# The load of x issued ahead of the opening barrier in a decode block

## Chip, cores, metric

The kernel runs on 1 core of one Trainium2 chip. The metric is the device time of one execution in microseconds (us). Runs within 1.5% of the fastest of their kernel count as fast runs.

## The reference

One decode step of a transformer block for two sequences, cut to what matters: attention with a cache of 8192 positions and 32 heads of 128, then a gated feed-forward layer.

```python
x = A_x                                                   # 2 x 1 x 512, bfloat16
h = x + attention(layernorm(x), k_cache, v_cache, wq, wo) # each cache 2 x 32 x 8192 x 128
return h + ffn(layernorm(h), W_gate, W_up, W_down)
```

The two caches are 268 of the 281 MB that the kernel reads. x is 2 KB, wq is 4 MB, and q = layernorm(x) @ wq is needed before any score can be computed.

## The kernel before

SyncE issues all big loads, in one queue, one after the other: wq, a piece of wo, K(0), V(0), K(1), V(1) and so on, 8 MB each, and at the end the feed-forward weights. The load of wq already stands ahead of the opening barrier, at which the five engines (SyncE, ScalarE, VectorE, TensorE and GpSimd) wait for one another after GpSimd has filled some constants. Each engine reports there with an instruction called a drain (in the trace of this kernel the last one, SyncE's, ends at 0.57 us, and the engines go on at 0.72 to 0.73); a small helper moves the instruction there in the built program. The load of x is issued by ScalarE behind the barrier.

```python
def ahead_of_barrier(emit, engine):
    block = nc.cur_bb.bb.instructions
    n = len(block)
    emit()
    new = block[n:]
    del block[n:]
    at = next(i for i, x in enumerate(block)
              if isinstance(x, mybir.InstDrain) and x.engine == engine)
    block[at:at] = new

ahead_of_barrier(lambda: nc.sync.dma_start(
    V[:, SLOT:], A_wq.rearrange("(p c) n -> p (c n)", c=DC)).then_inc(sem_wq, 16), nc.sync.engine)
nc.scalar.dma_start(x_row, A_x[:, 0]).then_inc(sem_x, 16)
nc.sync.dma_start(
    wo_rows, A_wo[128 * DR:].rearrange("(p r) n -> p (r n)", r=4)).then_inc(sem_wl, 16)
load(K, A_k_cache, 0, k_sem[0])
# ... GpSimd fills constants, among them:
pool.run(nc.gpsimd.memset(place, 0.0))                 # 128 x 2048
# ... VectorE, the layer norm of x:
dve.wait((sem_x, 16))
dve.run(nc.vector.bn_stats(out=bst[:], in_=x_row))
# ...
t_ln = dve.run(nc.vector.tensor_scalar(                # 2 x 512, the normalised x
    out=lnx_row, in0=x_row, scalar1=mv[:, 0:1], scalar2=sd[:, 0:1],
    op0=ALU.subtract, op1=ALU.mult))
# ... TensorE transposes x, VectorE copies it out (t_xlT), then q = layernorm(x) @ wq:
pe.wait((sem_wq, 16), t_xlT, t_zero)
# ... after the q matmuls (t_q), V(0) may overwrite wq:
sp.wait(t_q)
load(V, A_v_cache, 0, v_sem)
```

The softmax here doesn't subtract the row's maximum and nothing guards it: scores larger than these inputs give would overflow.

Of the kernel before, what the change touches and what calls it, by code (L numbers as in the profile page):

```python
# [39 lines left out]
def bass_sequential_preLN__gqa_block_cached__glu_gated_reglu__decode_kernel(  # L40
# [39 lines left out]
    with ExitStack() as es:  # L80
        def S(name):
            return es.enter_context(nc.semaphore(name))
# [17 lines left out]
        sem_x, sem_wq, sem_wl, sem_out = S("x"), S("wq"), S("wl"), S("out")  # L100
# [26 lines left out]
        x_row = kT[0][0:B, 0:D]  # L127
# [49 lines left out]
        if True:  # L177

            def program():
# [5 lines left out]
# [9 lines that stand above are left out]

                ahead_of_barrier(lambda: nc.sync.dma_start(
                    V[:, SLOT:], A_wq.rearrange("(p c) n -> p (c n)", c=DC)).then_inc(sem_wq, 16), nc.sync.engine)
                nc.scalar.dma_start(x_row, A_x[:, 0]).then_inc(sem_x, 16)
                nc.sync.dma_start(
                    wo_rows, A_wo[128 * DR:].rearrange("(p r) n -> p (r n)", r=4)).then_inc(sem_wl, 16)
                load(K, A_k_cache, 0, k_sem[0])  # L200
# [642 lines left out]
                nc.sync.wait_ge(sem_out, 16 * B)  # L843

            program()

    return nc
# [28 lines left out]
```

## Time and profile before

| | before |
|---|---|
| median of 6 runs beside the changed kernel | 656.74 us (656.60 to 657.23) |
| span of the profiled run | 655.6 us |
| bytes read from HBM, and their rate over the span | 281.05 MB, 429 GB/s |
| x landed, as VectorE saw it | 7.0 us |
| wq landed | 12.2 us |
| K(0) landed | 34.4 us |

The span is counted from the first instruction of the program; the time of an execution is about 1.2 us longer. x, wq and K(0) land in this order. The lines that carry this are in the prediction below. In them SPq and ACTq are loads being issued by SyncE and ScalarE; PE is TensorE (PEld its loads of weights), DVE VectorE, ACT ScalarE and POOL GpSimd; a bracket gives how long the engine was idle just before, and what ended that. Three dots mark rows left out. Two rows of the timeline that it doesn't show matter later (start, length, engine, line, operation): before the change, VectorE's TENSOR_SCALAR, the last step of the layer norm, ran beside GpSimd's copies, after GpSimd's memset (a fill with zeros) of 128x2048 had ended.

```profile
6.11 1.80 POOL L234 MEMSET prod<- 128x2048 bf16 x1
...
8.53 0.63 DVE L252 TENSOR_SCALAR kT<-kT,mv,sd 2x512 bf16<-2x512 bf16 x1
```

### The profile page before, as it was taken

How to read it: one execution, taken by the hardware profiler on the slowest of the kernel's cores; microseconds unless marked ns; L12 is line 12 of the kernel's file. 1: busy time of each engine (PE TensorE's matmuls, PEld its weight loads, DVE VectorE, ACT ScalarE, POOL GpSimd, SP SyncE). 2: the span in 40 equal slices, each digit the busy share in tenths (PEclk: the TensorE clock that was granted, in tenths of full speed). 3: DMA queues.
4: the chain of work that ended last, by engine and by line, in shares of the span. 5: the costliest groups of instructions: out<-in, count | busy, mean ns of one | idle time of the engine just before them, and what ended most of it. 6: DMA issues, size and time to landing. Idle time of an engine off the chain costs nothing.

```text
span 655.6 us, 8544 instructions
## 1 busy us (share of the span) xinstructions
PE 373.4 (57%) x3481; PEld 238.7 (36%) x3481; DVE 432.9 (66%) x275; ACT 304.7 (46%) x719; POOL 88.9 (14%) x96
## 2 busy tenths in 40 slices
PE   2374573747457374645638555474745637574677
PEld 0151441515234161523416143351614325151445
DVE  2187593947849395783939669393975939488771
ACT  1364362725536173453717445371653627254460
POOL 4000020030302103030120303003030300303000
PEclk9866557565665656566565656656565565657566
DMA  9999999999999999999999999999999999999997
GB/s 416 445 444 393 444 444 440 400 444 444 448 400 440 444 444 436 404 444 444 444 408 436 444 444 432 408 444 444 444 396 444 444 444 436 408 444 422 432 414 310
DMA packets 6324, 281.16 MB, mean 429 GB/s; under 512 B 710, under 2 KB 812, under 8 KB 1324
## 3 DMA queue, kind: packets, MB, share of 16 engines
q1 hardware_dynamic: 6308, 281.05, 99.4%
q8 instruction: 5, 0.08, 0.1%
q14 instruction: 3, 0.02, 0.0%
q10 hardware_dynamic: 8, 0.00, 0.0%
HBM read 281.05 MB, written 0.00 MB: 429 GB/s over the span
## 4 chain that ended last, share of the span: by engine, by line
DMA 64%; PE 24%; ACT 7%; DVE 4%; issue 1%; SPq 0%; DVEq 0%; ACTq 0%
DMA K<-in_A_k_cache_dram 59%; PE T L406 17%; ACT kT L589 7%; DMA V<-in_A_v_cache_dram 5%; PE S L389 5%; DVE prod L572 1%; DVE X L572 1%; PE O L429 1%; DVE X L563 1%; DVE prod L563 1%; DVE scores L577 0%; PE S L775 0%; PE O L775 0%; PE O L827 0%; ACT e L517 0%
## 5 line engine op out<-in xcount | busy, mean ns | idle before, releaser
L589 ACT ACTIVATE kT<-T 128x1024 bf16<-128x1024 bf16 x160 | 160.2, 1023 | 199.0 <-PE T L406 195.1
L406 PE MATMUL T<-ident_f,K 128*128 128x128 f32 x640 | 165.8, 424 | 100.4 <-DVEq L609 95.0
L563 DVE TENSOR_TENSOR X<-K,q_c 128x11264 bf16<-128x11264 bf16 x15 | 90.4, 6026 | 173.1 <-DMA K<-in_A_k_cache_dram 173.1
L429 PE MATMUL O<-V,e 128*16 128x512 bf16 x1024 | 116.0, 590 | 112.4 <-ACT e L517 79.6
L406 PEld LDWEIGHTS T<-ident_f,K 128*128 128x128 f32 x640 | 117.9, 217 | 102.6 <-DVEq L609 97.1
L572 DVE TENSOR_TENSOR prod<-prod 128x5632 bf16<-128x5632 bf16 (+1 forms) x68 | 104.3, 1533 | 4.0
L563 DVE TENSOR_TENSOR prod<-K,q_c 128x11264 bf16<-128x11264 bf16 x17 | 102.3, 6019 | 6.2 <-DMA K<-in_A_k_cache_dram 4.5
L517 ACT ACTIVATE e<-scores 32x88 bf16<-32x88 f32 x128 | 51.0, 399 | 103.2 <-DVEq L620 101.5
L429 PEld LDWEIGHTS O<-V,e 128*16 128x16 bf16 x1024 | 30.0, 115 | 184.5 <-ACT e L517 103.1
L572 DVE TENSOR_TENSOR X<-X 128x5632 bf16<-128x5632 bf16 (+3 forms) x60 | 92.0, 1533 | 3.7
L389 PE MATMUL S<-q_c,kT 128*128 128x8 bf16 x1280 | 60.9, 171 | 38.5 <-ACT kT L589 38.5
L389 PEld LDWEIGHTS S<-q_c,kT 128*128 128x128 bf16 x1280 | 52.0, 107 | 74.3 <-ACT kT L589 72.4
L544 POOL MEMSET O_l<- 128x32 bf16 x13 | 1.7, 131 | 427.7 <-DVEq L626 427.7
L549 POOL COPY rsel<-rows 128x112 bf16<-128x112 bf16 x14 | 40.4, 2885 | 39.6 <-DVEq L626 38.7
L442 PE MATMUL Ob<-sel,os_sb 128*128 128x4 f32 x136 | 27.7, 327 | 11.0 <-ACT os_sb L592 11.0
L517 ACT ACTIVATE e<-S 32x40 bf16<-32x40 f32 x128 | 31.9, 249 | 2.4 <-PE S L389 0.9
L442 PEld LDWEIGHTS Ob<-sel,os_sb 128*128 128x128 f32 x136 | 26.2, 287 | 13.3 <-ACT os_sb L592 13.2
L517 ACT ACTIVATION_READ_ACCUMULATOR e<-scores 32x1 f32 x128 | 28.0, 218 | 0.0
L517 ACT ACTIVATION_READ_ACCUMULATOR e<-S 32x1 f32 x128 | 25.6, 200 | 1.5
L551 POOL TENSOR_TENSOR O_l<-O_cur,mask 128x32 bf16<-128x32 bf16 x14 | 23.1, 1652 | 0.0
L560 POOL COPY q_c<-q_all 128x144 bf16<-128x144 bf16 x16 | 15.2, 951 | 44.6 <-PE O L429 33.6
L589 ACT ACT_TABLE_LOAD x15 | 19.2, 1283 | 0.3
(106 smaller groups left out, 137.8 us busy)
## 6 DMA issues: line engine op xcount, KB each, us to landing
K<-in_A_k_cache_dram SPq DMA_DIRECT2D x2, 4096.0 KB, 21.4
V<-in_A_wq_dram SPq DMA_DIRECT2D x1, 4096.0 KB, 12.2
V<-in_A_v_cache_dram SPq DMA_DIRECT2D x1, 4096.0 KB, 24.9
X<-in_A_wo_dram SPq DMA_DIRECT2D x1, 3584.0 KB, 18.0
V<-in_A_v_cache_dram SPq DMA_DIRECT2D x1, 3072.0 KB, 31.9
K<-in_B_W_up_dram SPq DMA_DIRECT2D x1, 1376.0 KB, 29.6
K<-in_B_W_gate_dram SPq DMA_DIRECT2D x1, 1376.0 KB, 32.5
V<-in_A_v_cache_dram SPq DMA_DIRECT2D x1, 1024.0 KB, 33.9
```

What stands on the lines that cost most here:

```text
L389: i = nc.tensor.matmul(Sp[p % 2][:, A * jj:A * jj + 2 * A], lhsT=kv_[:, k, r, :], rhs=q_c[:, 2 * A * r:2 * A * r + 2 * A], start=(r == 0), ...
L406: i = nc.tensor.transpose(Tp[g % 2][:, k * 128:(k + 1) * 128], k_t[:, j:j + 2, :].rearrange("p j d -> p (j d)").bitcast(F32), ident_f[:])
L429: i = nc.tensor.matmul(Op[0][c:c + 16, :], lhsT=e_t[q][:, j // VJ, :], rhs=v_t[:, j:j + VJ, :].rearrange("p j d -> p (j d)"), start=(q == ...
L442: i = nc.tensor.matmul(Ob[:, 0:A], lhsT=os_sb[:, jj * Dh:(jj + 1) * Dh], rhs=sel[:, A * jj:A * jj + A], start=(jj == 0), stop=(jj == VJ - 1))
L517: i = nc.scalar.activation(out=e_t[q][h, j0 // VJ:j1 // VJ, :].rearrange("p g (j a) -> p g j a", a=A)[:, :, :, a], in_=src(h, a), func=ACT ...
L544: pool.run(e.memset(o_window(o - 1)[0], 0.0))
L549: e.tensor_copy(out=rsel[:, :, o % B, :], in_=bass.AP(x.tensor, x.offset, [list(x.ap[0]), [DR - OS, A], [1, DR]]))
L551: e.tensor_tensor(out=w, in0=O_cur[:].unsqueeze(2).broadcast_to([128, A, NM]), in1=mask[:, off // 4:off // 4 + OS // 4 * (A - 1) + 1:OS // ...
L560: nc.gpsimd.tensor_copy(out=q_c[:], in_=q_all[:, o]).then_inc(g2d, 1)
L563: return nc.vector.tensor_tensor(out=pr[:, 0:JC, :], in0=tile(K, p)[:, 0:JC, :], in1=q_c[:, Q2:QW].unsqueeze(1).broadcast_to([128, JC, Dh] ...
L572: run(nc.vector.tensor_tensor(out=pr[:, 0:JC, 0:w], in0=pr[:, 0:JC, 0:w], in1=pr[:, 0:JC, w:2 * w], op=ALU.add))
L589: to_pe(nc.scalar.activation(out=kT[gg % 2][:], in_=Tp[gg % 2][:].bitcast(BF16), func=ACT.Copy))
```

## The change

The intent: x should go out at the same time as wq, not 0.8 us later, so that the layer norm is done earlier. The whole diff:

```diff
-                nc.scalar.dma_start(x_row, A_x[:, 0]).then_inc(sem_x, 16)
+                ahead_of_barrier(
+                    lambda: nc.scalar.dma_start(x_row, A_x[:, 0]).then_inc(sem_x, 16), nc.scalar.engine)
```

## The prediction

The forecast's sum is 656.6 us: the 656.61 us of the kernel before, with 0 from x, 0 from the barrier and at most 0 to 0.1 us for a later first packet of wq. A rival by which the issue of x delays that of wq, for an end at 656.8 to 657.0 us, is the +0.4 in the range. Of the sum, 0 to 0.1 us is the author's estimate, with no measurement behind it. The packet records are of the kernel before.

> **What bounds the kernel now.** I read the page's slices first, then the chain that ended last at its two ends, then the opening in order of time, and last the waits of the first 35 us. The page of the kernel before:
>
> ```profile
> span 655.6 us, 8544 instructions
> ...
> DMA  9999999999999999999999999999999999999997
> ...
> DMA 64%; PE 24%; ACT 7%; DVE 4%; issue 1%; SPq 0%; DVEq 0%; ACTq 0%
> ```
>
> The DMA row is 9 in 39 of 40 slices, the first included: one stream of loads runs from the start to almost the end, and the chain that ended last is DMA for 64%. Most of its other links only decide when the next load is issued. The chain at both ends of the loop:
>
> ```profile
> 1.19 33.17 DMA K<-in_A_k_cache_dram
> ...
> 47.34 25.73 DMA K<-in_A_k_cache_dram
> ```
>
> ```profile
> 551.14 25.16 DMA K<-in_A_k_cache_dram
> ...
> 608.73 31.88 DMA V<-in_A_v_cache_dram
> ```
>
> The columns are start, length, what. The first block of K lands at 1.19+33.17 = 34.36 us, the fifteenth at 551.14+25.16 = 576.30, so one of the 14 rounds between them takes 541.94/14 = 38.71 us. A round loads 8 MB of K and 8 MB of V, 16,777,216 bytes, which makes 433.4 GB/s. The loads keep ahead: V(0) is issued at 15.9, K(0) lands at 34.36, and 8 MB at that rate take 19.4 us, so V(0) lands near 53.7, while K(1) is already issued at 47.34. Each next load stands in the queue some 6 us before the one ahead of it is done. So the end is: the start of the stream, plus its bytes at 433 GB/s, plus the tail of TensorE and VectorE work after the last V has landed at 608.73+31.88 = 640.6, which is 15.0 us. The change can move the end through the start of the stream, through a break in it, or through the tail.
>
> The opening in order of time (start, length, engine, line, operation):
>
> ```profile
> 0.00 0.40 SPq L195 DMA_DIRECT2D V<-in_A_wq_dram  x1
> ...
> 0.80 0.34 SPq L198 DMA_DIRECT2D prod<-in_A_wo_dram  x1
> 0.80 0.55 ACTq L197 DMA_DIRECT2D kT<-in_A_x_dram  x1
> 1.19 0.46 SPq L182 DMA_DIRECT2D K<-in_A_k_cache_dram  x1
> ...
> 2.00 1.03 DVE L229 MEMSET O<- 128x512 f32 x2
> ...
> 7.01 0.68 DVE L242 BATCH_NORM_STATS2 bst<-kT 2x6 f32<-2x512 bf16 x1 [3.98 <-DMA kT<-in_A_x_dram]
> ...
> 9.74 0.17 DVE L265 COPY xlT<-T 128x16 bf16<-128x16 bf16 x1 [0.58 <-PE T L261]
> ...
> 12.26 3.58 PE L276 MATMUL O<-V,xlT 128*2 128x512 bf16 x32 [2.56 <-DMA V<-in_A_wq_dram]
> ...
> 24.20 0.10 PEld L362 LDWEIGHTS Ob<-ident,onesn 128*128 128x128 bf16 x1
> ```
>
> The load of wq goes out at 0.00, before the barrier; the load of x after it, at 0.80. VectorE waits 3.98 us for x. The normalised, transposed x is ready at 9.74+0.17 = 9.91, but TensorE starts the q matmuls only at 12.26, when wq has landed. And the last piece of the opening, at about 24.4, waits in turn for K. The waits of the first 35 us say the same:
>
> ```profile
> DVE X L563 <- DMA K<-in_A_k_cache_dram: 14.7, 1, 14.7
> ...
> DVE bst L242 <- DMA kT<-in_A_x_dram: 4.0, 1, 4.0
> ...
> PE O L276 <- DMA V<-in_A_wq_dram: 2.6, 1, 2.6
> ```
>
> The wait for x (4.0 us) lies inside the wait for wq, which ends later by 2.4 us, and that lies inside the wait for K, which ends later by 10 us.
>
> [...] its packet records show the two 1 KB packets of x at 5.27 and 5.37 us, 46 ns each, between 32 KB packets of wq of 1,213 ns, and the two 4-byte semaphore writes at 6.52 and 6.62, one more wq packet later. [...] both issues of 0.80 start together, the one on SyncE takes 0.34, that of the tiny x 0.55.
>
> **The change, part by part.** Nothing is added or removed. On ScalarE the x issue moves from behind the wait on the barrier to the place ahead of its drain; the other four engines keep their order, which the built order of both programs confirms.
> (1) ScalarE reaches its drain at 0.13 us in the trace, so x is issued at about 0.13 instead of 0.80, 0.67 us earlier. [...] I take the whole issue as the 0.55 us of today: done at about 0.68. [...]
> (2) The barrier. Today SyncE's drain is the last to end, at 0.57, and the engines leave at 0.72 to 0.73. ScalarE's drain now ends at 0.68 plus up to the 0.12 that SyncE's drain takes: 0.7 to 0.8. The engines should leave 0.1 to 0.25 us later, near 0.9, and the loads of wo and K with the first GpSimd memset come later by as much. The stream doesn't see it: wq's 4 MB keep the DMA engines busy to about 12.3, and the K issue at 1.19 has some 11 us of room. The GpSimd constants end at 9.5 and their last use begins at 19.8.
> (3) x's packets. wq's first packets start at 1.02 us, 1.0 us after their issue began. [...] with none to two wq packets ahead of them instead of three, and perhaps one before the semaphore write. At 1.2 us a packet x lands at 2 to 5 us, middle 3.5, against 7.01. VectorE is free at 3.03, so BATCH_NORM_STATS2 starts at about 3.5 and xlT is ready at 3.5+2.9 = 6.4, 3.5 us earlier.
> (4) What follows: the q matmuls still start at 12.26, since they need all of wq. The 3.5 us won become 3.5 us more of TensorE waiting. V(0) is issued at 15.9, K lands at 34.4: unmoved.
> (5) x's 2 KB at 433 GB/s are 5 ns, before and after.
> Sum on the path that sets the end: 0 from x, 0 from the barrier, and at most the delay of wq's first packet, which I put at 0 to 0.1 us. Predicted: 656.6 us.
>
> **The rivals.** [...] *The chain from x matters after all*: if the opening set the end, 3.5 us would be won, 653.1 us. Against it are two waits that end later, with 2.4 and 10 us of slack. *The barrier costs*: if a stage after it were tight, 0.1 to 0.25 us would be added, 656.8. Against it: nothing after the barrier is used within 10 us of being tight to the stream, save the x chain itself. *The time outside the span*: 656.61 is timed and 655.6 is the span; an earlier ScalarE instruction could shift what is counted by 0.1 us either way.
>
> **Range and chances.** The three runs before lie within 0.11 us, the profiled one read 656.9. The modelled effects are 0 to +0.4, and I allow 0.5 us for another chip: 656.1 to 657.1. A gain or loss of 2% is 13 us, which no part of the opening could give or take without breaking the stream. Faster 0.005, within 2% 0.985, slower 0.01.
>
> **What would show it right or wrong.** Right: the x issue starts near 0.1 us; the wait of BATCH_NORM_STATS2 shrinks from 3.98 us to under 2; the wait of the q matmuls for wq grows from 2.6 to about 6; they still start at 12.2 to 12.4; K(0) lands at 34.3 to 34.5 and the rounds keep 38.71 us. Wrong on a size: x lands as late as before, so its place among the packets isn't set by its issue time. Wrong as a whole: wq's landing moves by over 0.3 us, or the end moves without it.

## The result, and the profile after

The changed kernel took 656.73 us (median of 6 runs, 656.47 to 657.03), the kernel before 656.74 us in the same rounds. The ratio is 0.9999, with a 95% interval of 0.9986 to 1.0012. All ratios here are the mean time of one kernel's fast runs over that of the other's of the same rounds, so not quite the ratio of the medians quoted. The time is the same; the program, read from its page, is as full of loads as it was:

```profile
span 655.3 us, 8543 instructions
...
DMA  9999999999999999999999999999999999999997
```

The span is 0.3 us shorter here, but the spans of the six runs lie between 655.2 and 655.7, so this is scatter. What moved is in the opening. The timeline of the changed kernel:

```profile
0.00 0.40 SPq L195 DMA_DIRECT2D V<-in_A_wq_dram  x1
0.12 0.55 ACTq L198 DMA_DIRECT2D kT<-in_A_x_dram  x1
...
1.10 0.34 SPq L199 DMA_DIRECT2D prod<-in_A_wo_dram  x1
...
4.74 0.68 DVE L243 BATCH_NORM_STATS2 bst<-kT 2x6 f32<-2x512 bf16 x1 [1.42 <-DMA kT<-in_A_x_dram]
...
6.26 2.07 DVE L253 TENSOR_SCALAR kT<-kT,mv,sd 2x512 bf16<-2x512 bf16 x1
6.39 1.80 POOL L235 MEMSET prod<- 128x2048 bf16 x1
...
8.91 0.17 DVE L266 COPY xlT<-T 128x16 bf16<-128x16 bf16 x1 [0.58 <-PE T L262]
...
12.16 3.21 PE L277 MATMUL O<-V,xlT 128*2 128x512 bf16 x32 [3.29 <-DMA V<-in_A_wq_dram]
```

x is issued at 0.12 instead of 0.80 and seen at 4.74 instead of 7.01, so the early issue bought 2.27 us of arrival for 0.68 us of issue. The barrier opens 0.3 us later: the load of wo is issued at 1.10 instead of 0.80, because ScalarE comes to the barrier later (its drain starts at 0.72 instead of 0.13). Of the 2.27 us only 0.83 are left when the transposed x is ready (9.08 instead of 9.91), because one TENSOR_SCALAR now takes 2.07 us instead of 0.63. And none is left at the q matmuls: they start when wq has landed, at 12.16 against 12.26. The gain has turned into waiting, as TensorE's wait for wq says: 3.29 us in the last row against 2.56 before. The load of K(0), on the chain that ended last, is issued 0.3 us later and lands no later:

```profile
1.49 32.69 DMA K<-in_A_k_cache_dram
```

K(0) landed at 34.17 after and 34.37 before the change, K(1) at 72.89 and 73.07.

### The profile page after: what moved, and what is told of

It is laid out like the page before. It is cut to its first block, busy times and chain, and to the rows that moved or that the text cites. A ratio compares the mean times of both kernels' runs of the same rounds, so it can differ in the third digit from the quotient of the medians.

```text
span 655.3 us, 8543 instructions
## 1 busy us (share of the span) xinstructions
PE 370.5 (57%) x3480; PEld 236.9 (36%) x3481; DVE 434.3 (66%) x275; ACT 304.5 (46%) x719; POOL 88.7 (14%) x96
## 4 chain that ended last, share of the span: by engine, by line
DMA 64%; PE 22%; ACT 7%; DVE 6%; issue 1%; DVEq 0%; SPq 0%
DMA K<-in_A_k_cache_dram 59%; PE T L407 17%; ACT kT L590 7%; DMA K<-in_B_W_gate_dram 5%; PE S L390 5%; DVE prod L564 2%; DVE prod L573 1%; DVE X L573 1%; DVE X L564 1%; DVE scores L578 0%; PE O L776 0%; PE O L828 0%; DVEq L629 0%; DVEq L610 0%; DVE kT L836 0%
## 5 line engine op out<-in xcount | busy, mean ns | idle before, releaser
L430 PE MATMUL O<-V,e 128*16 128x512 bf16 x1024 | 114.4, 582 | 112.2 <-ACT e L518 78.9
```

What stands on the lines that cost most here:

```text
L430: i = nc.tensor.matmul(Op[0][c:c + 16, :], lhsT=e_t[q][:, j // VJ, :], rhs=v_t[:, j:j + VJ, :].rearrange("p j d -> p (j d)"), start=(q == ...
```

## The experiments

The theory: the end is set by one stream of loads. The opening matters only through the start of that stream and through V(0) and K(1), whose issue waits for it, and x is needed much later than it lands in either kernel. The rivals: x or the barrier does count, and two effects cancel; or the opening as a whole has no influence at all, which would make the result empty. Each kernel is shown as a change of the changed kernel, except where said; each was correct. Each time stands beside the kernel before in the same rounds on the same chip.

**after_again**: the changed kernel unaltered.

> The changed kernel unaltered, to see how far the same program scatters and to give the next three a neighbour on the same chip. Theory (the x chain ends long before it is needed): ratio to the kernel before 1.000 within 0.0005, about 656.7 us. Its trace repeats the chain of the first one: x lands near 4.7 us, the TENSOR_SCALAR of the layer norm takes about 2.1 us again (if that was chance it takes 0.63), q matmuls start near 12.2.

Measured: 656.71 us, before 656.58, ratio 1.0001 (0.9987 to 1.0015). The long TENSOR_SCALAR was there again with 2.07 us and x at 4.75, so it is no chance. The q matmuls start at 12.29, and K(0) lands at 34.41.

**wq_behind**: wq and x both behind the barrier, as an edit of the kernel before.

```diff
-                ahead_of_barrier(lambda: nc.sync.dma_start(
-                    V[:, SLOT:], A_wq...).then_inc(sem_wq, 16), nc.sync.engine)
+                nc.sync.dma_start(V[:, SLOT:], A_wq...).then_inc(sem_wq, 16)
```

> wq goes back behind the barrier, x too, so both are issued together there. Theory (the end follows the start of the stream one for one): the first issue is about 0.8 us later from the engines' start, so the time is 0.7 to 0.8 us longer than before, ratio 1.0011, about 657.4. Rival (the opening has slack for this too, and the end is set by waits inside the loop): ratio 1.000. It is also the check that a difference of 0.7 us can be seen at all.

Measured: 657.59 us (657.38 to 657.72) against 656.58, ratio 1.0014 (1.0000 to 1.0027). Its timeline:

```profile
0.81 0.40 SPq L195 DMA_DIRECT2D V<-in_A_wq_dram  x1
0.81 0.55 ACTq L197 DMA_DIRECT2D kT<-in_A_x_dram  x1
...
13.03 3.58 PE L276 MATMUL O<-V,xlT 128*2 128x512 bf16 x32 [7.59 <-DMA V<-in_A_wq_dram]
```

The stream starts 0.8 us later, wq lands 0.8 us later, and the end comes 0.9 us later by the ratio. This is the sensitive spot of the opening. The interval just touches 1, but the slowest of the nine runs before (657.05) is faster than the fastest of these five, so a difference of under 1 us can be seen. x, on the other hand, was complete at 2.15 us, the second earliest of all kernels here, and it bought nothing.

**x_first_sp**: x on SyncE, ahead of wq, meant to leave no packet of wq in front of it.

```diff
-                ahead_of_barrier(lambda: nc.scalar.dma_start(x_row, A_x[:, 0])..., nc.scalar.engine)
+                # ahead of the load of wq:
+                ahead_of_barrier(lambda: nc.sync.dma_start(x_row, A_x[:, 0])..., nc.sync.engine)
```

> x is issued on SyncE ahead of wq, both before the barrier, so x cannot be behind any packet of wq. Theory: x lands near 2 us, VectorE no longer waits for it, the q matmuls still wait for wq; wq's issue begins 0.3 to 0.5 us later and the whole stream with it, so the time is 0.3 to 0.5 us longer, ratio 1.0005 to 1.0008. Rival (an early x is worth something in itself): shorter than before by up to 3 us. [...]

Measured: 657.19 us (656.93 to 657.31) against 656.58, ratio 1.0007 (0.9994 to 1.0021). The interval contains 1, but four of the five runs were slower than all nine runs before, and the fifth than eight of them. Its timeline:

```profile
0.00 0.33 SPq L196 DMA_DIRECT2D kT<-in_A_x_dram  x1
0.39 0.36 SPq L197 DMA_DIRECT2D V<-in_A_wq_dram  x1
...
12.79 3.58 PE L277 MATMUL O<-V,xlT 128*2 128x512 bf16 x32 [7.00 <-DMA V<-in_A_wq_dram]
```

x was complete at 1.46 us, the earliest of all, and TensorE just waited 7 us for wq. wq's first packet started at 1.38 us instead of 1.02 to 1.04, and the end moved by some 0.5 us. So an early x is worth nothing, and the place ahead of wq seems to cost about as much as wq starts later. On ScalarE's queue x doesn't cost this: in the changed kernel x's issue overlaps wq's and wq's issue still takes 0.40 us, with its first packet at 1.04.

**barrier_late**: eight more loads of x into an unused buffer stand ahead of the barrier (VectorE's wait for them, ahead of the loop, is left out here).

```diff
+                for n in range(8):
+                    ahead_of_barrier(lambda: nc.scalar.dma_start(
+                        X[0:B, n * D:n * D + D], A_x[:, 0]).then_inc(sem_pad, 16), nc.scalar.engine)
```

> Eight more 2 KB loads of x, into a buffer not yet used, stand in ScalarE's program ahead of the barrier behind the load of x; the barrier opens at about 4 us instead of 1.0. Theory (what stands behind the barrier is needed only when wq's 4 MB have drained at about 12 us): ratio 1.000 within 0.0005. Rival (the later barrier of the change costs one for one and a gain from x hides it): 3 us longer, ratio 1.0045.

Measured: 656.76 us against 656.58, ratio 1.0003 (0.9989 to 1.0016).

```profile
0.72 2.56 ACTq L202 DMA_DIRECT2D X<-in_A_x_dram  x8
3.79 1.28 ACT L254 ACT_TABLE_LOAD   x1 [3.79 <-PEq L867]
3.79 0.34 SPq L204 DMA_DIRECT2D prod<-in_A_wo_dram  x1
...
12.67 3.58 PE L282 MATMUL O<-V,xlT 128*2 128x512 bf16 x32 [4.24 <-DMA V<-in_A_wq_dram]
```

The barrier opened 3 us late, ten times the delay that the change causes, without a loss of 3 us. So the later barrier of the change isn't a cost that a gain from x hides.

**x_when_wq_landed**: x much too late, to find where it begins to count.

```diff
-                ahead_of_barrier(lambda: nc.scalar.dma_start(x_row, A_x[:, 0])..., nc.scalar.engine)
+                act.wait((sem_wq, 16))
+                nc.scalar.dma_start(x_row, A_x[:, 0]).then_inc(sem_x, 16)
```

> ScalarE issues x only when wq has landed, at about 12.2 us; its packets then stand behind 64 KB packets of K, so x lands at 20 to 25 us instead of 4.7, and the whole opening ends at 33 to 39 us instead of 24. Theory (the end is set by the stream; the next load of K is issued 6 us before it is needed): even if the loop starts up to 4 us late the stream doesn't run dry, ratio 1.000 within 0.001. Rival (the slack ends where K(0) lands, 34.4 us, and from there each us of the opening counts): up to 4 us longer, ratio up to 1.006.

Measured: 657.46 us (656.93 to 658.92, 4 runs) against 656.69, ratio 1.0018 (1.0002 to 1.0035). x was seen at 20.72 instead of 4.74, the opening ended at 35.68, after K(0) had landed. The run with the profile took 656.93; in it V(0) is issued at 27.15 and K(1) at 48.69, and V(0) and K(1) land at 53.51 and 72.86, no later than before. The issue of x shows something else:

```profile
12.45 0.55 ACTq L198 DMA_DIRECT2D kT<-in_A_x_dram  x1
```

It takes 0.55 us with no other issue near it, as it does beside wq's issue at 0.12 and beside wo's at 0.80. But two of the four runs were a microsecond or two longer, and the mean is outside the theory's 0.001 and inside the rival's range. So it was run again:

> The same kernel as x_when_wq_landed, whose four runs lay between 656.93 and 658.92 us, wider than any other, with the fastest one profiled. If the late opening costs nothing and the two long runs were chance, ratio 1.000 within 0.0005. If an opening that ends 1 us after K(0) has landed does cost, ratio 1.001 to 1.003 again, and a profile of a longer run should show the stream of loads with a gap that the kernel before doesn't have: between V(0) and K(1), or at K(2).

Measured: 657.03 us (656.61 to 658.36, 5 runs) against 656.86, ratio 1.0010 (0.9997 to 1.0024). Three runs at 656.6 to 657.0, two at 657.9 and 658.4, and again a short one profiled.

> The kernel of x_when_wq_landed a third time, one look only, to catch a profile of one of its long executions (4 of 9 so far were over 657.5 us). If it is long, the profile should show the stream with a gap beside V(0) or K(1), or a slower round later; if it is short again, what made the long ones long stays open.

Measured: 656.65 us, one run, short again, before 656.62. An x that comes 16 us late can thus be hidden: 5 of the 10 runs lie within 0.4 us of the kernel before. But 4 runs lost 1.0 to 2.2 us, and by the two ratios the mean loss is 0.7 to 1.2 us, so here the slack is nearly used up. Why those runs were long stays open: no profile of one was caught.

**x_after_k**: x in SyncE's queue behind K(0).

```diff
-                ahead_of_barrier(lambda: nc.scalar.dma_start(x_row, A_x[:, 0])..., nc.scalar.engine)
                 load(K, A_k_cache, 0, k_sem[0])
+                nc.sync.dma_start(x_row, A_x[:, 0]).then_inc(sem_x, 16)
```

> x stands in SyncE's program behind the load of K(0) and lands with it at about 34.4 us. Theory: the chain x, layer norm, q, loop start, which takes some 15 us, now starts at 34.4 and V(0), which goes into wq's place, is issued only near 41 us; the stream runs dry for 7 to 8 us and perhaps 2 us more before K(1): 664 to 668 us, ratio 1.011 to 1.017. Rival (the opening never matters): 1.000. Rival (every us of the 30 by which x is late counts): 687 us, ratio 1.045.

Measured: 668.46 us (667.78 to 670.91) against 656.69, ratio 1.0186 (1.0162 to 1.0210). This is 11.8 us longer and a little above the range that I gave, although x was seen at 32.65 and V(0) issued at 39.08, each some 2 us earlier than I expected. First the SyncE rows of its timeline, then its table of two stretches (start and end, length, busy time and instructions of PE, PEld, DVE, ACT and POOL, granted clock, share of the DMA engines, GB/s; a packet counts whole in the stretch in which it starts, so a share can pass 1), then the same stretches before:

```profile
39.08 0.34 SPq L182 DMA_DIRECT2D V<-in_A_v_cache_dram  x1
61.05 0.33 SPq L182 DMA_DIRECT2D K<-in_A_k_cache_dram  x1
```

```profile
32.00:40.00 8.00, 4.05 (x42) 1.42 (x43) 2.40 (x7) 0.80 (x2) 0.00 (x0) 1.00 0.00 0
58.00:62.00 4.00, 2.43 (x40) 1.81 (x38) 3.85 (x2) 3.24 (x4) 0.00 (x0) 0.67 0.14 53
```

```profile
32.00:40.00 8.00, 5.29 (x43) 4.46 (x44) 5.51 (x1) 3.77 (x4) 0.00 (x0) 0.50 1.06 459
58.00:62.00 4.00, 0.29 (x8) 0.00 (x0) 3.78 (x4) 0.03 (x1) 0.00 (x0) 0.84 1.17 508
```

The stream is dry twice: for 7.5 us until V(0) comes, and again before K(1), which is issued when V(0) is nearly through. The packet records add up: the packets of all 16 engines took 653.9 us a head against 651.8 before, and the rest of the span, without packets, was 13.6 us against 3.8. So 9.8 us of the 11.9 us by which the spans differ are dry stream, and 2.1 us are packets that took longer, which I hadn't reckoned with. The packet records say which: those with which V(0) and K(1) start after the two breaks, near 40.0 and 62.0 us, and V(1), issued only at 80.94, near 82.0. These first 64 KB packets of the engines took 2.7 to 3.5 us instead of 2.42, together 1.9 us a head. The opening does matter, but only once the next load of the stream comes late, and far less than the 28 us by which x was late.

**x_third_in_line**: as x_when_wq_landed, with two small loads ahead of x in its queue (the wait for them is left out).

```diff
                 act.wait((sem_wq, 16))
+                for n in range(2):
+                    nc.scalar.dma_start(X[0:B, n * D:n * D + D], A_x[:, 0]).then_inc(sem_pad, 16)
                 nc.scalar.dma_start(x_row, A_x[:, 0]).then_inc(sem_x, 16)
```

> As x_when_wq_landed, but two 2 KB loads into an unused buffer are issued ahead of x on the same queue, so that x should stand behind two more 64 KB packets of K and land 2 to 5 us later, near 23 to 25.5 us; the opening then ends at 37.5 to 40 and K(1) is issued at 50 to 53 us instead of 47.3. V(0)'s data are through near 51.2 us (it is seen as landed 53.6, one packet of 2.4 us later) and K(1)'s packets start 1 us after its issue. Theory (the edge is where the next load is issued later than 1 us before the one ahead is through): the stream has a gap of 0 to 3 us between V(0) and K(1), the time is 0.5 to 3 us longer, ratio 1.001 to 1.005. Rival (each us of the opening past the landing of K(0) counts, from 33 us on): 5 to 7 us longer, ratio 1.008 to 1.011.

Measured: 667.31 us (666.38 to 668.84) against 656.62, ratio 1.0162 (1.0148 to 1.0176). The dose was not what I meant to give: x came at 30.57 instead of 20.72, not 2 to 5 but 9.85 us later, so neither number of the expectation can be held against it. With x at 30.57, V(0) was issued at 37.01 and K(1) at 61.14, and no packet ran for 5.5 us from 32.45 and for 2.1 us from 60.0. The opening ended at 48.44, and K(0) had landed at 32.96: if each us past that landing counted, as the rival has it, some 15 us would have been lost, not 10.7. So the edge lies between an x at 20.7 us, which can be hidden but no longer always is, and one at 30.6, which loses 10.7 us; the change moves x from 7.0 to 4.7, far inside. Why x came so late is read from its packet records: on x's queue the data of each small load started at 17.48, 22.36 and 27.24 us and its 4-byte semaphore writes at 19.94, 24.82 and 29.69 (the first engine). In these records one item went per 64 KB packet of the big queue (2.42 us), and each small load had two, its data and its semaphore write (the count that the waiting engine waits for; VectorE began at 30.57, after the last one at 29.69): 2 loads x 2 items x 2.44 us = 9.8 us.

**place_after_ln**, **memset_split** and **memset_split_wait**: where the TENSOR_SCALAR lost its 1.4 us. In the first, GpSimd waits for the layer norm before it builds the constants `pick` and `place`.

```diff
-                pool.wait(t_ident)                      # ahead of the layer norm in the program
+                pool.wait(t_ident, t_ln)                # behind it
                 pool.run(nc.gpsimd.tensor_copy(out=pick...
                 pool.run(nc.gpsimd.memset(place, 0.0))
```

> GpSimd builds pick and place only after the layer norm, so that its memset of 128x2048 no longer runs beside VectorE's TENSOR_SCALAR. Theory (the TENSOR_SCALAR took 2.07 us instead of 0.63 [...]): it takes 0.63 again and the transposed x is ready 1.4 us sooner, near 7.6 us; the time stays, ratio 1.000 within 0.0007. Rival (packets of wq or the late landing of x slow it): it stays near 2.07.

In the second and third the memset is split:

```diff
-                pool.run(nc.gpsimd.memset(place, 0.0))
+                for n in range(4):
+                    pool.last()                         # only in memset_split_wait
+                    pool.run(nc.gpsimd.memset(place[:, n], 0.0))
```

> The same memset as four of a quarter each, at the same place. Theory [...]: VectorE waits for the rest of one quarter at most, the TENSOR_SCALAR takes 0.7 to 1.2 us. Rival (it is slowed by all of GpSimd's writing while it lasts, or by the DMA): it stays near 2.07. The time stays, ratio 1.000 within 0.0007.

> The memset in four quarters as in memset_split, but each waits for the one ahead of it to have finished, which leaves a gap between them. Theory ([...] back to back memsets overlap by 60 ns and leave none): VectorE gets in after the first quarter, the TENSOR_SCALAR takes 0.7 to 1.2 us instead of 2.3. Rival (GpSimd [...] slows VectorE, as long as it has memsets to run): 2.2 us or more. The time stays, ratio 1.000 within 0.0007.

Measured: 656.71 against 656.69 us (ratio 1.0001), 656.54 against 656.69 (0.9998), 656.62 against 656.86 (0.9996), all with intervals of about 0.0016 to either side: the time stays. The three timelines, one fence each in the order named:

```profile
6.24 0.40 DVE L242 TENSOR_SCALAR kT<-kT,mv,sd 2x512 bf16<-2x512 bf16 x1
...
7.11 1.80 POOL L251 MEMSET prod<- 128x2048 bf16 x1
```

```profile
6.14 2.31 DVE L254 TENSOR_SCALAR kT<-kT,mv,sd 2x512 bf16<-2x512 bf16 x1
6.39 1.92 POOL L236 MEMSET prod<- 128x512 bf16 x4
```

```profile
6.43 0.73 DVE L255 TENSOR_SCALAR kT<-kT,mv,sd 2x512 bf16<-2x512 bf16 x1
6.50 2.29 POOL L237 MEMSET prod<- 128x512 bf16 x4
```

Without GpSimd beside it the TENSOR_SCALAR takes 0.40 us, so even the 0.63 of before, beside GpSimd's copies, was longer than that. My expectation for the plain split fell: the TENSOR_SCALAR didn't end after a quarter but behind all four, and took 2.31 us. The four memsets of 0.53 us start 0.47 us apart, so each starts before the one ahead has ended. With waits between them it ended behind the first one: that memset ends at 7.03 and the TENSOR_SCALAR at 7.16. The 0.14 us between these two ends is the same behind the last of the four in memset_split (8.31 and 8.45) and behind the one memset of the changed kernel (8.19 and 8.33). In the changed kernel GpSimd was first: its copy, from 6.05 to 6.45, was running when the TENSOR_SCALAR began at 6.26. So the four memsets back to back held the TENSOR_SCALAR up like one (2.31 us), and with waits between them only the first did (0.73 us). Their overlap alone doesn't explain it: in the kernel before, GpSimd's copies overlap too, yet the TENSOR_SCALAR ended behind the third of the four (9.02 and 9.16), while the fourth ran from 8.82 to 9.49. Why stays open, and by what GpSimd holds VectorE up, no run shows.

## Why the prediction was right, point by point

The time was right and so was the reason for it; some sizes on the way were off, and one was right by luck.

1. The issue: predicted at about 0.13 us for 0.55 us; it was 0.12 and 0.55. The 0.55 was right by luck: the prediction laid it to wq's issue beside it (a cause that no trace shows), but x_when_wq_landed has 0.55 us with no other issue near. In all eleven timelines read in which ScalarE issues x, the first load that it issues took 0.55 us (in x_third_in_line that isn't x, and x took 0.28); in barrier_late the eight that followed took 0.24 to 0.36 us (2.56 for all). wq's issue kept its 0.40 us and its first packet started at 1.04 instead of 1.02. So the allowance of 0 to 0.1 us for a delay of wq's first packet held, and the rival that x's issue delays wq's by 0.2 to 0.4 us is out; x_first_sp, with wq's first packet at 1.38 us, shows what that rival would have looked like.
2. The barrier: predicted 0.1 to 0.25 us later, measured 0.3. The mis-sized term is the end of ScalarE's drain, put at 0.7 to 0.8; it started at 0.72, took 0.14 (before the change 0.01) and ended at 0.86. That it costs nothing is shown by barrier_late (3 us later, ratio 1.0003).
3. x's arrival: predicted between 2 and 5 us, middle 3.5, with none to two wq packets ahead of the data and perhaps one before the semaphore write; measured 4.74, with one 32 KB packet ahead of each, where three went ahead of the data before, which is how 0.68 us became 2.27 (data at 2.94 and 3.11, semaphore writes at 4.20 and 4.36).
4. The transposed x: predicted at 6.4, measured 9.08. Of the 2.7 us missed, 1.2 are the arrival and 1.4 are the step "xlT is ready at 3.5+2.9", which carried over a TENSOR_SCALAR of 0.63 us to a time at which GpSimd's memset runs. It took 2.07. place_after_ln (0.40) and memset_split_wait (0.73) show the cause, GpSimd's memset.
5. The q matmuls: predicted at 12.26, measured 12.16 and 12.29. Their wait for wq was predicted to grow from 2.6 to about 6, it grew to 3.3 and 3.4; this is the same missed term as in 4. In place_after_ln it is 5.2. Two of the signs named for "right" were missed by little: the start at 12.16 lies under 12.2 to 12.4, and K(0) at 34.17 under 34.3 to 34.5; in after_again both lie inside.
6. The sum on the path that sets the end, 0: measured ratio 0.9999. The sensitivity that it rests on was tested both ways: a start of the stream 0.8 us later costs 0.9 us, an x as early as 1.46 us gains nothing, and an x as late as 20.7 us can go unnoticed in half of the runs.

One statement of the prediction was wrong without harm: that after the last V at 640.6 a tail of 15.0 us of TensorE and VectorE work follows. The stream doesn't end there. The feed-forward weights are behind V in the queue, and the last of them, 96 KB of W_down, is issued at 619.56 and lands 33.6 us later, at 653.2. The tail behind the stream is 2.4 us, and the DMA row's 7 in its last slice fits that. The rows for that last piece in the kernel before, from the timeline and from the table of loads (size, us from issue to landing):

```profile
619.56 5.81 SPq L726 DMA_DIRECT2D wd_last<-in_B_W_down_dram  x1
```

```profile
wd_last<-in_B_W_down_dram SPq DMA_DIRECT2D x1, 96.0 KB, 33.6
```

No version here beats the two kernels: the shortest medians, 656.54 and 656.62, lie within the scatter of the kernel before, whose single runs went from 656.46 to 657.23 and whose medians over five sets from 656.58 to 656.86.

## What to carry to other kernels

Before a load is moved forward, find the load that its user waits for last: an operand that comes early only lengthens the wait for the other one (here from 2.56 to 3.29 us). In a kernel like this one, whose DMA row is full from end to end, only what starts the stream, breaks it or trails it counted, and slack can be measured by delaying the thing on purpose until the time moves. And when something moves to another time, look at what runs beside it there: a duration read from the old place may not hold in the new one (here 0.63 us became 2.07).
